# Sixteen unread products of the identity on TensorE in a fused attention and mixing kernel

## Chip, cores and metric

One core of a Trainium2 chip runs the whole kernel. The metric is the device time of one execution in microseconds, as the median of several runs.

## What is computed

Three parts follow each other: a blockwise attention over 2 batches, 8 heads, 768 positions and 64 values a head; a channel mix with a gate; and a token and channel mix. Everything is float32.

```python
# attention: a local window of 15 keys on each side, and 24 block summaries
scores = concat(where(|i - j| < 16, q k^T / 8, -1e9), q kmax^T / 8 + log(32))
a = softmax(scores)
x = a @ concat(v, vmean)
# channel mix
xk = mu_k * x + (1 - mu_k) * x_prev ;  xr = mu_r * x + (1 - mu_r) * x_prev
y = sigmoid(xr @ w_r) * (relu(xk @ w_k)**2 @ w_v)
# token mix and channel mix
u = y + (relu(y^T @ w_tok1) @ w_tok2)^T
out = u + relu(u @ w_ch1) @ w_ch2
```

## The kernel before

Attention is cut into 24 units: batch `b`, tile `t` of 128 queries, and `e`, which takes the even or the odd heads. A unit passes through four stages, each with its own place in the loop of `attention()`:

- `s_stage` (line 288): 8 score products on PE (`sp`, fp32, 64 rows, 120 columns) into a PSUM bank of tag `s` (2 of them); then for each of four head pairs DVE adds the mask and takes the minimum (`sm`, `mn`, line 307) and ACT takes the exponential (`pe`, line 310).
- `n_stage` (line 315), one unit later: DVE takes the reciprocal of the sums (`den`), POOL multiplies the four `pe` tiles (line 320).
- `t_stage` (line 323), two units later: four transposes on PE (`pt`, line 326), and a copy to `PT` by DVE in batch 0 and by ACT in batch 1.
- `v_stage` (line 334), three units later: 8 products on PE (`pv`, line 343); after the odd unit of a tile ACT copies the result to `xT` (line 348).

Between the units stands the first part of the channel mix, the generator `main()`. It handles 256 positions at a time: `mixed` makes the mixed input in two parts, high and low (`tmp` on POOL line 417, `xk` on DVE line 418, `xh` on ACT, `xl` on DVE line 420); `mm3` multiplies three times for each pair of parts (line 428), into `ko` for `w_k`, one PSUM bank of tag `ko`, and into `acc` for `w_v`. `k2_tile` squares the result in between. The weights come in as 8-byte numbers and are split by ACT, DVE and POOL (`Weights.step`, lines 133 to 158); a step is taken in every third turn of the loop from the tenth.

How attention and `main()` interleave in the program is set by a credit: each `yield` of `attention()` gives its cost times 1.2 (1.8 from the 25th on), and products of `main()` are emitted until it is used up. A scheduler then fixes the order of every engine, by priorities (`ahead`) and readiness on a timeline of its own. A product, copy or transfer can be tied with `after` behind the last score product so far (`mark`), in the order of the queues alone.

In front of the loop SP issues the loads, POOL makes the identity `ident` (line 78) and the masks, DVE takes block maxima of the keys (`ks`, line 221) and sums of the values (`vrs`, line 243), and POOL copies the maxima next to the keys (`kw`, line 227). The first score product waits for the last of these.

Behind attention come the rest of `main()`, the gate (`ro`), the token mix (`h`, `ho`) and the channel mix (`go`, `o`), which are products of 128x512 one behind the other.

Of the kernel before, what the change touches and what calls it, by code (L numbers as in the profile page):

```python
# [25 lines left out]
RATIO, NR, RATIO2 = 1.2, 25, 1.8  # L26
SIDE_EVERY = 3
AHEAD = 4
WFIRST = 2
S2COST, S3COST, S4COST = 4, 5, 4  # L30
PT_ACT = (1,)
# [18 lines left out]
def fused_kernel(ctx, tc, q, k, v, vt, mu, w_k, w_v, w_r, w_t1, w_t2, w_c1, w_c2, out):  # L50
    nc = tc.nc
# [21 lines left out]
    def bank(tag, bufs, shape, name):  # L73
        return ps.tile(shape, F32, tag=tag, bufs=bufs, name=name)

    const = pool("const", "left")
    ident = const.tile([128, 128], F32, name="ident")
# [14 lines left out]
    class Slot:  # L92


        def __init__(self, pl, tag):
            self.pl, self.tag = pl, tag
# [16 lines left out]
    class Weights:  # L113


        def __init__(self):
            self.todo, self.loaded, self.rounded, self.pin, self.ahead = [], [], [], 0, AHEAD

# [43 lines left out]
    def behind(inst, marks):  # L162

        for m in marks:
            tc.add_manual_dep(inst.ins, m.ins.name,
                              mybir.DependencyInfo(mybir.DependencyClass.NoSync, mybir.DependencyReason.DATA), reason="queue order")

    def after(inst):

        behind(inst, mark[-1:])  # L170
# [19 lines left out]
    def ahead(n):  # L190

        def wrap(fn):
            def run(*args, **kw):
                with tc.high_priority(n) if n else ExitStack():
                    return fn(*args, **kw)
            return run
        return wrap
# [3 lines left out]
    def st_of(b):  # L201
        if b not in state:
            state[b] = {"kw": {}, "qT": {}, "vw": {}, "pv": {}}
            state[b]["ks"] = at.tile([128, NP, NB], F32, tag="ks", bufs=2, name="ks")
        return state[b]
# [17 lines left out]
    @ahead(HK)  # L223
    def kw_sums(b, t):
        st = state[b]
        for o in (0, WC - NB):
            nc.gpsimd.tensor_scalar(st["kw"][t][:, :, o:o + NB], st["ks"], 1.0, 1.0, ALU.mult, ALU.mult)
# [17 lines left out]
    @ahead(HR)  # L245
    def v_gather(b):
        st = state[b]
        vp = bank("pt", 2, [128, NP, 128], "vp")
        for p in range(NP):
            nc.tensor.transpose(vp[:NB, p], st["vr"][:, p], ident)  # L250
        st["vs"] = at.tile([NB, DM], F32, tag="vs", bufs=1, name="vs")
        nc.scalar.activation(st["vs"], vp[:NB].rearrange("p g e -> p (g e)"), AF.Copy, scale=1.0 / BLOCK)

    @ahead(HL)
    def vw_load(b, t):
        ws = []
        for half in range(2):
            w = ybuf[:NC, 2 * t + half] if b == 0 else at.tile([NC, DM], F32, tag="vw", bufs=6, name="vw")
            row, srow = (NB, 0) if half == 0 else (0, NK)
            key = 128 * t + 64 * half  # L260
            after(nc.sync.dma_start(w[row:row + NK], v[b, key:key + NK]))
            ws.append((w, srow))
        st_of(b)["vw"][t] = ws

    def vw_sums(b, t):
        ahead(HV if b or t == 0 else 0)(copy_sums)(b, t)
# [12 lines left out]
    @ahead(HL)  # L279
    def q_load(b, t):  # L280
        if b == 0:
            st_of(b)["qT"][t] = xT[:, :, XB + 1 + 128 * t:XB + 129 + 128 * t]
        else:
            st_of(b)["qT"][t] = at.tile([128, NP, 128], F32, tag="qT", bufs=QB, name="qT")
        after(nc.sync.dma_start(st_of(b)["qT"][t], q[b, t]))

    @ahead(HS)
    def s_stage(u):
        b, t, e = u
        st = state[b]  # L290
        mask = masks[1 if t == 0 else 2 if t == NT - 1 else 0]
        kw, qT = st["kw"][t], st["qT"][t]
        sp = bank("s", 2, [128, NP, NC], "sp")
        mn = at.tile([128, NP], F32, tag="mn", bufs=3, name="mn")
        den = at.tile([128, NP], F32, tag="den", bufs=4, name="den")
        P = []
        r = slice(64 * e, 64 * e + 64)
        for p in range(NP):
            for half in range(2):
                c0 = half * (WC - NC)  # L300
                m = nc.tensor.matmul(sp[64 * half:64 * half + 64, p], qT[r, p, 64 * half:64 * half + 64],  # L301
                                 kw[r, p, c0:c0 + NC], start=True, stop=True)
        if PINL:
            mark.append(m)
        for p in range(NP):
            s = at.tile([128, NC], F32, tag="sm", bufs=4, name="sm")
            nc.vector.tensor_tensor_reduce(out=s, in0=sp[:, p], in1=mask, op0=ALU.add, op1=ALU.min,  # L307
                                           scale=-1.0 / math.sqrt(D), scalar=3.0e38, accum_out=mn[:, p:p + 1])
            pe = at.tile([128, NC], F32, tag="pe", bufs=12, name="pe")
            nc.scalar.activation(pe, s, AF.Exp, bias=mn[:, p:p + 1], scale=-1.0, accum_out=den[:, p:p + 1])  # L310
            P.append(pe)
        return {"u": u, "P": P, "den": den}

    @ahead(HN)
    def n_stage(z):
        den = z["den"]
        nc.vector.tensor_scalar(den, den, 1e-9, None, ALU.add)
        nc.vector.reciprocal(den, den)
        for p in range(NP):
            nc.gpsimd.tensor_scalar(z["P"][p], z["P"][p], den[:, p:p + 1], 1.0, ALU.mult, ALU.mult)  # L320

    @ahead(HT)
    def t_stage(z):
        pt = bank("pt", 2, [128, NP, 128], "pt")
        for p in range(NP):
            nc.tensor.transpose(pt[:NC, p], z["P"][p], ident)  # L326
        z["PT"] = at.tile([NC, NP, 128], F32, tag="PT", bufs=2, name="PT")
        if z["u"][0] in PT_ACT:
            nc.scalar.copy(z["PT"], pt[:NC])
        else:  # L330
            nc.vector.tensor_copy(z["PT"], pt[:NC])

    @ahead(HV)
    def v_stage(z):
        b, t, e = z["u"]
        st = state[b]
        if e == 0:
            st["pv"][t] = bank("pv", 1, [128, NP, 128], "pv")
        pv = st["pv"][t]
        for p in range(NP):  # L340
            h = 2 * p + e
            for half in range(2):
                nc.tensor.matmul(pv[64 * e:64 * e + 64, p, 64 * half:64 * half + 64],  # L343
                                 st["vw"][t][half][0][:, h * D:(h + 1) * D],
                                 z["PT"][:, p, 64 * half:64 * half + 64], start=True, stop=True)
        if e == 1:
            c0 = b * XB + 1 + 128 * t
            nc.scalar.copy(xT[:, :, c0:c0 + 128], pv)
# [5 lines left out]
    def attention():  # L354
        zs = {}
        for i in range(n_units + VLAG):
            if i < n_units:
                b, t, e = units[i]
                zs[i] = s_stage(units[i])
                yield 0.95  # L360
                if e == 1 and t + 1 < NT:
                    kw_sums(b, t + 1)
                if t == 0 and e == 1 - b:
                    if b == 0:
                        v_gather(b)
                    vw_sums(b, 0)
            if 0 <= i - 1 < n_units:
                n_stage(zs[i - 1])
            if 0 <= i - TLAG < n_units:
                t_stage(zs[i - TLAG])  # L370
                yield 0.43
            if 0 <= i - VLAG < n_units:
                v_stage(zs.pop(i - VLAG))
                yield 0.7
                done_tiles[0] = (i - VLAG + 1) // 2
            if i < n_units:
                if e == 0:
                    if t + 1 < NT and t + 1 not in state[b]["vw"]:
                        vw_load(b, t + 1)
                    if b and t + 2 < NT:  # L380
                        q_load(b, t + 2)
                elif t + 1 < NT:
                    vw_sums(b, t + 1)
                if b + 1 < B:
                    prep_next(b + 1, 2 * t + e)
# [113 lines left out]
    def drain(g):  # L499
        for _ in g:  # L500
            pass


    q_load(0, 0)
    for t in range(NT):
        k_load(0, t)
# [7 lines left out]
    for t in range(2, NT):  # L514
        for _ in range(WFIRST):
            weights.load()
# [36 lines left out]
    for n, cost in enumerate(attention()):  # L553
        weights.pin = PIN0 if n < N0 else PIN1
        if n >= W0 and n % SIDE_EVERY == 0:
            weights.step()
        credit += cost * (RATIO if n < NR else RATIO2)
        while credit > 0:
            got = next(hidden, None)
            if got is None:  # L560
                credit = 0.0
                break
            credit -= got
# [246 lines left out]
```

## Time and profile before

| | us |
|---|---|
| median of 3 runs (531.76 to 535.03) | 532.42 |
| the profiled execution | 532.74 |
| its span, first to last instruction | 530.9 |
| PE busy in the span | 504.5 |
| DVE, ACT, POOL busy | 253.5, 204.1, 203.2 |

Busy time of PE is from the start of a product to its modelled end, so groups overlap a little and a busy PE need not be at its peak. A product in fp32 leaves more than one record in the trace; these are called passes below. Times in rows count from the start of the span.

### The profile page before, as it was taken

How to read it: one execution, taken by the hardware profiler on the slowest of the kernel's cores; microseconds unless marked ns; L12 is line 12 of the kernel's file. 1: busy time of each engine (PE TensorE's matmuls, PEld its weight loads, DVE VectorE, ACT ScalarE, POOL GpSimd, SP SyncE). 2: the span in 40 equal slices, each digit the busy share in tenths (PEclk: the TensorE clock that was granted, in tenths of full speed). 3: DMA queues.
4: the chain of work that ended last, by engine and by line, in shares of the span. 5: the costliest groups of instructions: out<-in, count | busy, mean ns of one | idle time of the engine just before them, and what ended most of it. 6: DMA issues, size and time to landing. Idle time of an engine off the chain costs nothing.

```text
span 530.9 us, 7836 instructions
## 1 busy us (share of the span) xinstructions
PE 504.5 (95%) x2936; PEld 412.2 (78%) x2936; DVE 253.5 (48%) x556; ACT 204.1 (38%) x471; POOL 203.2 (38%) x298
## 2 busy tenths in 40 slices
PE   1899979999999999999999999999999999999995
PEld 1676867788888898888877788888888888888884
DVE  3976997614222466668854957443331221211112
ACT  0666656545443545455435435343310110110100
POOL 6567798934344555557741522422200000000000
PEclk9999999999999999999999999999999999999999
DMA  8999732102100850000145733000020000200002
GB/s 269 323 308 374 228 94 66 38 8 71 39 2 1 279 197 1 1 1 2 40 129 170 294 123 115 1 1 1 0 80 0 2 0 1 79 0 1 0 1 79
DMA packets 24197, 45.40 MB, mean 86 GB/s; under 512 B 2112, under 2 KB 11328, under 8 KB 24160
## 3 DMA queue, kind: packets, MB, share of 16 engines
q1 hardware_dynamic: 24160, 44.90, 26.3%
q8 instruction: 23, 0.38, 0.3%
q14 instruction: 14, 0.11, 0.1%
HBM read 41.16 MB, written 3.15 MB: 83 GB/s over the span
## 4 chain that ended last, share of the span: by engine, by line
PE 77%; DVE 9%; POOL 5%; issue 4%; ACT 2%; DMA 2%; SPq 1%; POOLq 0%; DVEq 0%; ACTq 0%
PE o L735 19%; PE go L428 19%; PE ko L428 9%; PE acc L428 8%; PE sp L301 5%; PE pv L343 4%; PE ro L428 4%; PE pt L326 3%; PE ho L428 3%; PE h L428 2%; POOL pe L320 1%; DMA xT<-in_vt_dram 1%; DVE xk L418 1%; DVE wf L147 1%; POOL tmp L417 1%
## 5 line engine op out<-in xcount | busy, mean ns | idle before, releaser
L428 PE MATMUL go<-u,w 128*128 128x512 f32 x432 | 106.7, 393 | 0.0
L156 POOL TENSOR_TENSOR w<-wf,w 128x512 fp32r<-128x512 f32 x50 | 66.1, 1325 | 88.0 <-ACT w L155 86.6
L428 PEld LDWEIGHTS go<-u,w 128*128 128x128 f32 x432 | 80.7, 188 | 17.5
L735 PE MATMUL o<-w,gh 128*128 128x512 f32 x288 | 89.0, 395 | 0.0
L650 DVE SCALAR_TENSOR_TENSOR gl<-go,gh 128x512 fp32r<-128x512 f32 x36 | 24.9, 691 | 121.1 <-ACT gh L649 121.0
L428 PE MATMUL ko<-xh,w 128*128 128x256 f32 x384 | 77.7, 288 | 0.0
L649 ACT ACTIVATE gh<-go 128x512 fp32r<-128x512 f32 x36 | 21.5, 597 | 128.8 <-PE go L428 128.7
L428 PEld LDWEIGHTS ko<-xh,w 128*128 128x128 f32 x384 | 62.1, 189 | 2.7 <-issue 0.9
L735 PEld LDWEIGHTS o<-w,gh 128*128 128x128 f32 x288 | 54.0, 188 | 12.1
L428 PE MATMUL acc<-w,kh 128*128 128x512 f32 x192 | 60.9, 401 | 0.6 <-ACT kh L442 0.6
L320 POOL TENSOR_SCALAR pe<-pe,den 128x120 f32<-128x120 f32 x96 | 46.2, 497 | 26.2 <-ACT rl L440 15.1
L735 PE MATMUL o<-w,gl 128*128 128x512 f32 x144 | 55.4, 394 | 0.0
L428 PE MATMUL ko<-xl,w 128*128 128x256 f32 x192 | 54.8, 286 | 0.1
L155 ACT CAST w<-wf 128x512 fp32r<-128x512 f32 x50 | 30.9, 618 | 52.0 <-DVE wf L153 49.6
L310 ACT ACTIVATE pe<-sm,mn 128x120 f32<-128x120 f32 x96 | 36.8, 385 | 33.9 <-DVE mn L307 27.8
L153 DVE SCALAR_TENSOR_TENSOR wf<-wst,wf 128x512 int32<-128x512 int32 x50 | 44.0, 882 | 8.9 <-ACT wst L143 6.8
L417 POOL TENSOR_SCALAR tmp<-xT,oms 128x256 f32<-128x256 f32 x52 | 32.9, 642 | 29.9 <-DVE xk L418 25.2
L443 POOL TENSOR_TENSOR kl<-rl,kh 128x512 fp32r<-128x512 f32 x24 | 33.5, 1396 | 21.6 <-ACT kh L442 13.0
L428 PEld LDWEIGHTS acc<-w,kh 128*128 128x128 f32 x192 | 34.4, 189 | 7.8 <-ACT kh L442 1.0
L418 DVE SCALAR_TENSOR_TENSOR xk<-xT,mus,tmp 128x256 f32<-128x256 f32 x52 | 34.7, 697 | 10.9 <-POOL tmp L417 10.8
L428 PE MATMUL acc<-w,kl 128*128 128x512 f32 x96 | 37.5, 402 | 0.9 <-POOL kl L443 0.9
L428 PEld LDWEIGHTS ko<-xl,w 128*128 128x128 f32 x192 | 36.2, 189 | 1.5 <-DVE xl L420 0.3
(77 smaller groups left out, 719.9 us busy)
## 6 DMA issues: line engine op xcount, KB each, us to landing
wst<-in_moe_w_ch_dram SPq DMA_DIRECT2D x24, 512.0 KB, 5.1
wst<-in_moe_w_k_dram SPq DMA_DIRECT2D x8, 512.0 KB, 9.4
wst<-in_moe_w_v_dram SPq DMA_DIRECT2D x8, 512.0 KB, 7.2
kw<-in_k_dram SPq DMA_DIRECT2D x12, 320.0 KB, 4.4
wst<-in_moe_w_tok_dram SPq DMA_DIRECT2D x6, 512.0 KB, 5.3
out_dram<-o SPq DMA_DIRECT2D x12, 256.0 KB, 2.1
ybuf<-in_v_dram SPq DMA_DIRECT2D x12, 192.0 KB, 10.6
vw<-in_v_dram SPq DMA_DIRECT2D x12, 192.0 KB, 2.8
```

The source lines that it names most:

```text
L153: nc.vector.scalar_tensor_tensor(wi, top, 3, wi, ALU.logical_shift_left, ALU.bitwise_or)
L155: self.rounded.append(nc.scalar.copy(hi, wf))
L156: nc.gpsimd.tensor_tensor(lo, wf, hi.bitcast(F32), ALU.subtract)
L301: m = nc.tensor.matmul(sp[64 * half:64 * half + 64, p], qT[r, p, 64 * half:64 * half + 64], kw[r, p, c0:c0 + NC], start=True, stop=True)
L310: nc.scalar.activation(pe, s, AF.Exp, bias=mn[:, p:p + 1], scale=-1.0, accum_out=den[:, p:p + 1])
L320: nc.gpsimd.tensor_scalar(z["P"][p], z["P"][p], den[:, p:p + 1], 1.0, ALU.mult, ALU.mult)
L417: nc.gpsimd.tensor_scalar(tmp, xT[:, d, x0 - 1:x0 - 1 + MW], om[:, d:d + 1], 1.0, ALU.mult, ALU.mult)
L418: nc.vector.scalar_tensor_tensor(xk[:, d], xT[:, d, x0:x0 + MW], mu[:, d:d + 1], tmp, ALU.mult, ALU.add)
L428: nc.tensor.matmul(o, l, r, start=(first and i == 0), stop=(last and i == 3 * n - 1))
L443: nc.gpsimd.tensor_tensor(lo, rl, hi.bitcast(F32), ALU.subtract)
L650: nc.vector.scalar_tensor_tensor(lo, o, 0.0, hi.bitcast(F32), ALU.max, ALU.subtract)
L735: nc.tensor.matmul(acc[t], l, r, start=(f == 0 and i == 0), stop=(f == nf - 1 and i == 2))
```

## The change

A function `spin(n)` is new. It takes the bank of tag `ko`, which `main()` uses later, and multiplies the identity by the identity, repeated four times, in fp32: 128 rows, 512 columns. Nothing reads the result. Eight of these are emitted ahead of all loads, and one more behind the scores of each of the first eight units. Each is tied with `after` behind the last score product so far; for the first eight there is none yet.

```diff
+SPIN0 = 8
+SPIN, SPIN_UNITS = 1, 8
...
                 zs[i] = s_stage(units[i])
+                if i < SPIN_UNITS:
+                    spin(SPIN)
                 yield 0.95
...
-
+    def spin(n):
+
+        o = bank("ko", 1, [128, 4, 128], "spin")
+        for _ in range(n):
+            after(nc.tensor.matmul(o, ident, ident.unsqueeze(1).to_broadcast([128, 4, 128]), start=True, stop=True))
+
+
+    spin(SPIN0)
     q_load(0, 0)
```

Line numbers shift by 2 in `attention()` and the functions above it, by 4 behind it and by 11 behind `spin`.

The start of PE's program before: the scores of the first two units (`sp_230`, `sp_257`), the sums of the values being transposed (`vp`), and two more units.

```order
L301 MATMUL sp_230<-kw_90,xT_84 64x120
L301 MATMUL sp_257<-kw_90,xT_84 64x120
L301 MATMUL sp_230<-kw_90,xT_84 64x120 x7
L301 MATMUL sp_257<-kw_90,xT_84 64x120 x7
L250 MATMUL vp_286<-ident_61,vrs_224 24x128 x2
L301 MATMUL sp_303<-kw_92,xT_84 64x120 x8
```

The same place now, up to the third of the single products.

```order
L511 MATMUL spin_88<-ident_61 128x512 x8
L303 MATMUL sp_239<-kw_99,xT_84 64x120
L303 MATMUL sp_268<-kw_99,xT_84 64x120
L303 MATMUL sp_239<-kw_99,xT_84 64x120 x7
L303 MATMUL sp_268<-kw_99,xT_84 64x120 x4
L511 MATMUL spin_266<-ident_61 128x512
L303 MATMUL sp_268<-kw_99,xT_84 64x120 x3
L252 MATMUL vp_299<-ident_61,vrs_233 24x128 x2
L303 MATMUL sp_316<-kw_101,xT_84 64x120 x8
L511 MATMUL spin_295<-ident_61 128x512
L303 MATMUL sp_358<-kw_101,xT_84 64x120 x8
L511 MATMUL spin_343<-ident_61 128x512
```

(A second pair of `vp`, which stands ahead of `sp_358`, is left out.) The eight stand ahead of everything, and single ones between the scores of the first units. All sixteen stand ahead of the first `ko` of `main()`.

Further on the order of PE is another one too. In batch 1, around the scores of its third tile, it was this before (`sp_1579` and `sp_1670` are scores, `acc` and `ko` products of `main()`):

```order
L428 MATMUL acc_1424<-w_773,kh_1417 128x512 x2
L428 MATMUL acc_1424<-w_773,kl_1418 128x512
L301 MATMUL sp_1579<-kw_785,qT_1215 64x120 x8
L301 MATMUL sp_1670<-kw_980,qT_1387 64x120
L326 MATMUL pt_1709<-ident_61,pe_1489 120x128
L428 MATMUL ko_1606<-xh_1152,w_1036 128x256
```

Now the scores of the third tile (`sp_1604`) stand here:

```order
L328 MATMUL pt_1467<-ident_61,pe_1259 120x128
L303 MATMUL sp_1604<-kw_810,qT_1240 64x120 x6
L328 MATMUL pt_1467<-ident_61,pe_1263 120x128
L303 MATMUL sp_1604<-kw_810,qT_1240 64x120 x2
L345 MATMUL pv_1477<-PT_1379,vw_1120 64x64
L345 MATMUL pv_1477<-PT_1379,vw_1122 64x64
```

Where products of `main()` stood on both sides of these scores, there are now transposes and value products of other units: batch 1 stands closer together, and more of `ko` and `acc` stands behind it.

## Rows read from the trace of the kernel before

**Rows 1.** The page's part 2: the span in 40 slices, busy tenths and granted clock.
```profile
PE   1899979999999999999999999999999999999995
PEclk9999999999999999999999999999999999999999
```

**Rows 2.** Windows by stage; columns as the heading row names them.
```profile
core 0: us, PE busy (x) PEld busy (x) DVE busy (x) ACT busy (x) POOL busy (x), PEclk, DMA share, GB/s
21.80:38.00 16.20, 15.75 (x111) 12.31 (x111) 12.47 (x42) 10.26 (x35) 12.85 (x25) 1.00 1.08 317
38.00:58.30 20.30, 20.01 (x128) 14.44 (x128) 15.13 (x60) 13.68 (x45) 16.29 (x25) 1.00 0.90 300
58.30:62.50 4.20, 4.20 (x60) 3.73 (x60) 4.20 (x13) 3.16 (x11) 3.58 (x6) 1.00 0.91 306
62.50:87.70 25.20, 22.14 (x200) 18.53 (x198) 22.44 (x57) 13.50 (x34) 20.25 (x31) 1.00 0.48 128
87.70:184.70 97.00, 96.32 (x770) 78.28 (x769) 38.23 (x140) 48.31 (x142) 52.19 (x81) 1.00 0.18 58
```

**Rows 3.** Timeline of PE: start, length in us, instruction, passes, [idle before].
```profile
53.99 3.31 PE L343 MATMUL pv<-PT,ybuf 120*64 120x64 f32 x32
57.23 1.11 PE L326 MATMUL pt<-ident,pe 128*120 128x128 f32 x4
...
59.39 1.15 PE L343 MATMUL pv<-PT,ybuf 120*64 120x64 f32 x16
60.47 0.65 PE L326 MATMUL pt<-ident,pe 128*120 128x128 f32 x4
...
62.54 0.36 PE L428 MATMUL ko<-xh,w 128*128 128x256 f32 x1
...
69.99 0.85 PE L326 MATMUL pt<-ident,pe 128*120 128x128 f32 x3 [1.56 <-DVE den L317]
70.77 1.15 PE L343 MATMUL pv<-PT,ybuf 120*64 120x64 f32 x16
...
90.23 0.33 PE L326 MATMUL pt<-ident,pe 128*120 128x128 f32 x1
```

**Rows 4.** The chain that ended last: start, us on it, what.
```profile
21.83 0.47 PE pt L326
22.30 1.80 PE sp L301 x16
...
32.00 1.90 PE pv L343 x16
...
51.06 0.63 DVE PT L331
...
97.19 0.56 PE sp L301 x8
...
108.82 1.07 PE pv L343 x16
```

**Rows 5.** The chain from 21.8 to 51.1 us, shares by line.
```profile
by line: PE sp L301 42.0%; PE pv L343 29.3%; PE pt L326 20.8%; DVE PT L331 4.2%; DVE wf L153 2.1%; issue 1.8%; DVE sm L307 1.0%; ACT pe L310 0.7%; DVE mn L307 0.0%
```

**Rows 6.** Groups on PE from 21.8 to 58.3 us: passes, busy us, mean ns, idle before.
```profile
L301 PE MATMUL sp<-kw,xT 64*64 64x120 f32 x112 | 15.6, 416 | 0.0
L343 PE MATMUL pv<-PT,ybuf 120*64 120x64 f32 x96 | 12.5, 320 | 0.7 <-DVE PT L331 0.7
L326 PE MATMUL pt<-ident,pe 128*120 128x128 f32 x31 | 10.7, 444 | 0.3 <-POOL pe L320 0.3
```

**Rows 7.** Timeline of the first 15 us: identity, first scores, first sum of values.
```profile
1.11 0.29 POOL masks.py:199 TENSOR_SCALAR_AFFINE_SELECT ident<-ident 128x128 f32<-128x128 f32 x1
...
11.73 2.95 PE L301 MATMUL sp<-kw,xT 64*64 64x120 f32 x32 [11.73 <-POOL kw L227]
...
13.38 1.75 DVE L243 TENSOR_REDUCE vrs<-xT 128x48 f32<-128x1536 f32 x1 [2.14 <-DMA xT<-in_vt_dram]
```

**Rows 8.** Waits of DVE from 21.8 to 62.5 us: us in total, times, longest.
```profile
DVE PT L331 <- PE pt L326: 4.6, 2, 2.4
DVE sm L307 <- ACT pe L310: 3.6, 3, 2.8
```

## The prediction

> **What bounds the kernel now.** I read the page's parts 1 and 2 first, then windows by stage, then the PE timeline where its durations change, and then the chain of waits. PE is busy for nine tenths or more of nearly every slice behind the first, and its clock row shows the same top digit in all 40 [rows 1]. [...] The reader is to distrust that row here, because the durations on PE do not fit it. Sixteen passes of `pv` take 1.90 us in the chain at 32.00 us and 1.07 us at 108.82 us; sixteen passes of `sp` take 1.80 us at 22.30 us, and eight take 0.56 us at 97.19 us [rows 4]. The change falls between two neighbours of one kind: four `pt` take 1.11 us at 57.23 us and 0.65 us at 60.47 us, and `pv` x16 at 59.39 us is already short [rows 3]. A single `pt` takes 0.47 us early [rows 4] and 0.33 us late [rows 3], a good part of it a fixed latency, so the step of one more is (1.11 - 0.47)/3 = 0.213 us against (0.65 - 0.33)/3 = 0.107 us: a factor of two, which is the distance between the two clock levels. So I read it thus: PE runs at the low level from its first product to about 58.3 us and at the high one from there on. Transfers do not explain it: the DMA share is 0.90 in the slow stage before 58.3 us and 0.91 in the fast one behind it [rows 2].
>
> What PE did before the rise: it was busy for 20.01 of 20.30 us [rows 2], with products on 64 columns and transposes, and the last thing of note is a run of 32 `pv` [rows 3]. So mere occupancy did not raise the clock in this kernel.
>
> [...]
>
> Then the chain. From 21.8 to 51.1 us it lies on PE: `sp`, `pv` and `pt` hold 42.0 + 29.3 + 20.8 = 92% of these 29.3 us, or 27.0 us [rows 5]. At 51.06 us it goes over to DVE [rows 4], which has the first mixed tile to make; the first dense `ko` product starts at 62.54 us [rows 3]. From 87.7 to 184.7 us PE is busy 96.32 of 97.00 us [rows 2]; a shift that arrives there lasts to the end.
>
> **The front: eight products.** They wait for the identity alone, whose last step begins at 1.11 us and takes 0.29 us [rows 7], so they start near 1.5 us. No row shows a full 128x512 fp32 product. By the step of `pt` (128 columns in one pass, 0.213 or 0.107 us) 512 columns take 0.85 or 0.43 us a pass; the trace shows two passes for each fp32 `sp` product (32 passes for 16 instructions [rows 7]), so I take 1.71 us slow and 0.86 us fast for one. At one pass it would be half of that; two fits the other fp32 products of the kernel. Eight then take 6.9 us (all fast) to 13.7 us (all slow): they end at 8.4 to 15.2 us, and at 11.8 us if half of their work is fast. The first `sp` starts at 11.73 us today [rows 7], so half-fast is free. All slow would hold `sp` for 3.5 us, but DVE is in a 1.75 us reduction until 15.1 us [rows 7] and starts on the scores only then, so that at most some 2 us would reach the chain. I take 0, with 2 us as the other end.
>
> **The eight further products.** In the new order of PE eleven of the sixteen stand ahead of the first `pt`: the front and three more. There the chain runs over DMA, DVE, ACT and POOL, and PE has room (it is not on the chain until 21.83 us [rows 4]); I cost these three at nothing, and at 2.6 us if that cover is gone. The other five lie in the stretch where PE is the chain: 5 x 0.86 = 4.3 us fast, 8.6 us slow. Each writes the bank of `ko` and is read by nobody; the first real `ko` stands behind all sixteen, so no `ko` waits for a reader of theirs.
>
> **What the clock gives back.** Between 21.8 and 58.3 us the trace has 112 passes of `sp`, 96 of `pv` and 31 of `pt` [rows 6]. With steps from the chain [rows 4]: `sp` 0.1125 - 0.070 = 0.0425 us x 112 = 4.8 us; `pv` 0.119 - 0.067 = 0.052 us x 96 = 5.0 us; `pt` 0.213 - 0.107 = 0.106 us x 31 = 3.3 us. Sum 13.1 us of PE work in a stretch where PE is busy 35.8 us [rows 2]. On the chain are 27.0 of these: 13.1 x 27.0/35.8 = 9.9 us. Less the five products, 9.9 - 4.3 = 5.6 us. If all of it counted (PE alone is the limit up to 58.3 us), it would be 13.1 - 4.3 = 8.8 us.
>
> **Whether the others can follow.** In 21.8 to 62.5 us DVE waited 4.6 us for `pt` and 3.6 us for `pe` [rows 8], together 8.2 us; POOL was busy 12.85 + 16.29 of 36.5 us up to 58.3 us [rows 2], so it has 7.4 us. Both have more than 5.6 us and less than 8.8 us: the room bears the first figure and not the second. The stretch behind it, 62.5 to 87.7 us, holds DVE at 22.44 and POOL at 20.25 of 25.2 us [rows 2]; nothing is won there, but a start 5.6 us earlier is kept if the work ahead of it is the same.
>
> **The order.** It is not the same. The scheduler places batch 1 earlier on PE: between the twelfth and the twenty-second unit's `pv` there stand 108 `ko` and 36 `acc` products, where before there were 204 and 104. Ahead of the first `xl` DVE has 6 weight splits instead of 8, and 6 key reductions instead of 9. All of it has to be done before the dense stage anyway, so I count 0, with a loss of up to 8 us (the rival below) and a gain of up to 3 us (idle time of PE in 62.5 to 87.7 us [rows 2] that better filling could close) as the ends.
>
> **Sum.** The profiled execution took 532.74 us, of which 530.9 us are the span; the median of the three runs shown is 532.42 us, 0.3 us less, so the sum may be read against either. 532.74 - 5.6 = 527.1 us.
>
> **Rivals.** *All of the low clock comes back.* If DVE and POOL fill their waits fully and the filling behind improves by those 3 us, the gain is 8.8 + 3 = 12 us: 521 us. For it: no engine has more busy time up to 58.3 us than PE. Against it: DVE and POOL have only 8.2 and 7.4 us to give, at different moments.
>
> *The gain is hidden.* DVE carries the chain from 51.06 us; if it is the limit earlier too, its waits turn from waits for PE into waits for ACT's `pe` and POOL, and 1 us remains: 532 us. For it: the 3.6 us of waits for `pe` are not PE's own [rows 8].
>
> *The clock does not rise, or falls back between units.* Then each of the eight costs 1.71 us: 8.6 us in the PE stretch plus some 1 us at the start, 542 us. Place: PE, 21.8 to 51.1 us. It decides if four `pt` still take 1.11 us in that stretch. For it: the products between the spins are the ones that did not raise the clock before. Against it: once up, it stayed up over a PE wait of 1.56 us; the `pv` behind that wait are short again [rows 3].
>
> [...] The pause between the front and the first `sp` is up to 3.3 us by the ends above; no run here shows a pause of that length in the fast stage.
>
> *The bunched batch 1 costs more than the clock gives.* In 62.5 to 87.7 us, where attention is dense, PE idles 3.06 of 25.2 us, 12%; behind it 0.68 of 97 us [rows 2]. If 12% holds for the next 70 us of the new order, that is 8.3 us more; with half the gain, 532.74 - 2.8 + 8.3 = 538 us. It decides if PE's idle time from 90 to 160 us is over 6 us.
>
> **How the numbers follow.** 1% is 5.3 us, about what a measurement of this kernel can tell from no change. Chances: the forecast (gain of 3 to 9 us) 0.45, all comes back 0.18, hidden 0.17, clock low 0.10, bunching 0.10. Faster by over 1%: some 0.30 of the forecast's 0.45, and the 0.18: 0.48. Slower by over 1%: the last two but for a little, 0.18. Within 1%: 0.34. The range reaches from 518 us (all comes back and some more) to 539 us (bunching in full); the forecast's own range is 523.5 to 530 us.
>
> **What would show it.** In the changed profile: the first eight products from about 1.5 us, the later of them half as long as the first; four `pt` in 0.65 us from the first unit on; sixteen `sp` passes in some 1.1 us (twice the 0.56 us of eight) at 22 us; the first `ko` near 57 us and not 62.54 us; from 190 us on the same rows as before, some 5 to 6 us earlier. The prediction is wrong if `pt` is still long after 12 us, if the first `ko` comes no earlier, or if it comes earlier and PE then stands idle between 80 and 160 us.

## The result and the profile after

The changed kernel takes 521.15 us (median of 4 runs, 520.51 to 521.76); the kernel before took 532.76 us beside it (4 runs). The ratio is 0.9772, 95% interval 0.9754 to 0.979: 11.6 us less, about twice the 5.3 us (1%) that the prediction puts as what a measurement can tell from no change. The forecast was 527.1 us; the direction was right, and the size is that of the first rival (521 us). Where executions of one kernel below spread by more than 1.5%, its ratio counts those near its fastest alone, and the median counts all.

The profiled execution took 520.51 us, its span is 518.7 us, 12.2 less than before. The page's part 2 of the changed kernel, which answers to [rows 1]:

```profile
PE   8997889999999999999999999999999999999995
PEclk9899999999999999999999999999999999999998
```

PE now works from the first slice on. Its clock row shows one step down in the second slice and one in the last, where the row before had none at all; and yet this is the kernel with the faster PE. The timeline of PE says why (start, length in us, instruction, passes, [idle before]); it answers to [rows 3, 7]:

```profile
1.46 9.96 PE L511 MATMUL spin<-ident 128*128 128x512 f32 x16 [1.46 <-POOL ident masks.py:199]
11.84 1.33 PE L303 MATMUL sp<-kw,xT 64*64 64x120 f32 x26 [0.42 <-POOL kw L229]
...
15.31 0.39 PE L252 MATMUL vp<-ident,vrs 128*24 128x128 f32 x2 [0.53 <-DVE vrs L245]
16.27 1.04 PE L303 MATMUL sp<-kw,xT 64*64 64x120 f32 x16 [0.57 <-issue]
17.23 1.92 PE L511 MATMUL spin<-ident 128*128 128x512 f32 x2
18.95 0.63 PE L252 MATMUL vp<-ident,vrs 128*24 128x128 f32 x2
19.51 1.67 PE L303 MATMUL sp<-kw,xT 64*64 64x120 f32 x16
21.11 1.13 PE L511 MATMUL spin<-ident 128*128 128x512 f32 x2
22.07 0.38 PE L328 MATMUL pt<-ident,pe 128*120 128x128 f32 x2
22.39 1.04 PE L303 MATMUL sp<-kw,xT 64*64 64x120 f32 x16
23.35 0.65 PE L328 MATMUL pt<-ident,pe 128*120 128x128 f32 x4
...
27.04 1.90 PE L345 MATMUL pv<-PT,ybuf 120*64 120x64 f32 x32
...
53.52 0.39 PE L432 MATMUL ko<-xh,w 128*128 128x256 f32 x1 [0.82 <-ACT xh L423]
...
191.82 1.11 PE L432 MATMUL ro<-w,xh 128*128 128x512 f32 x4
```

Sixteen `sp` passes take 1.04 us where they held the chain for 1.80 [rows 4], four `pt` 0.65 where they took 1.11, 32 `pv` 1.90 where they took 3.31 [rows 3]. Only from 17.4 to 20.9 us are they long again (`sp` 1.67 us, a single product 1.92). The front itself, cut where the trace records its first change of clock (7.19 us), the products alone:

```profile
core 0: us, PE busy (x) PEld busy (x), PEclk, DMA share, GB/s
1.40:7.19 5.79, 5.73 (x7) 2.52 (x8) 1.00 0.86 247
7.19:11.50 4.31, 4.23 (x10) 1.52 (x8) 1.00 1.14 327
```

Seven passes fill the first 5.73 us, 0.82 us each; ten fill 4.23 us, 0.42 us each. The clock column says 1.00 on both sides of a factor of two: it shows the fall that comes later in this execution (0.51 from 17.40 to 20.90 us, below), and not the low level at which the execution begins. That is how the clock row of before could show nothing of a PE that ran at half speed from 11.73 to 58.6 us (the step of one `pt` more was 0.213 us, and 0.107 us behind it). Whoever reads that row reads durations beside it.

By stage (columns as in [rows 2]):

```profile
17.40:20.90 3.50, 3.50 (x18) 1.86 (x20) 2.60 (x21) 2.93 (x14) 0.89 (x4) 0.51 1.10 321
...
21.80:53.50 31.70, 27.22 (x306) 19.68 (x303) 26.56 (x118) 24.29 (x84) 27.84 (x50) 1.00 1.07 335
...
53.50:80.00 26.50, 23.29 (x206) 19.07 (x207) 25.58 (x56) 17.04 (x46) 24.99 (x37) 1.00 0.64 178
80.00:191.80 111.80, 111.80 (x887) 95.58 (x886) 50.87 (x152) 58.08 (x152) 64.16 (x86) 1.00 0.23 80
```

The 12.2 us are made in two places. The first `ko` starts at 53.52 us and not at 62.54 [rows 3], 9.0 us earlier. From there to the first `ro` it is 191.82 - 53.52 = 138.3 us, and was 141.4 (that `ro` started at 203.97): 3.1 us less, in a stretch that was already at the high level before. Behind it both kernels need the same 327 us.

The first part can be taken apart. From 21.8 us to the first `ko` there were 40.70 us with PE busy 15.75 + 20.01 + 4.20 = 39.96 [rows 2]; there are 31.70 with PE busy 27.22. The groups on PE in the two stretches (passes, busy us, mean ns, idle before), first from 21.8 to 62.5 us of before, where [rows 6] end at 58.3, then from 21.8 to 53.5 us now:

```profile
L301 PE MATMUL sp<-kw,xT 64*64 64x120 f32 x128 | 16.4, 398 | 0.0
L343 PE MATMUL pv<-PT,ybuf 120*64 120x64 f32 x128 | 14.8, 296 | 0.7 <-DVE PT L331 0.7
L326 PE MATMUL pt<-ident,pe 128*120 128x128 f32 x38 | 11.9, 415 | 0.3 <-POOL pe L320 0.3
```

```profile
L345 PE MATMUL pv<-PT,ybuf 120*64 120x64 f32 x128 | 8.7, 225 | 3.7 <-DVE PT L333 2.8 <-ACT wst L145 0.9
L303 PE MATMUL sp<-kw,xT 64*64 64x120 f32 x128 | 8.1, 270 | 0.0
L328 PE MATMUL pt<-ident,pe 128*120 128x128 f32 x38 | 6.8, 286 | 0.0
L511 PE MATMUL spin<-ident 128*128 128x512 f32 x12 | 6.7, 636 | 0.0
```

So both stretches hold the same work, but for the products. The chain of waits in the new one, by line:

```profile
by line: POOL pe L322 26.9%; PE spin L511 19.4%; issue 13.4%; PE sp L303 11.7%; POOL w L158 7.9%; PE pv L345 5.8%; POOL tmp L421 5.5%; PE pt L328 3.6%; DVE sm L309 3.4%; DVE PT L333 1.9%; ACT pe L312 1.6%; DVE den L320 0.3%; DVE den L319 0.
```

PE held 92% of the chain [rows 5]. Now POOL holds the largest share, and PE's largest is that of the products themselves: 19.4% of 31.7 us, 6.1 us. Without them PE's busy time is 27.2 - 6.1 = 21.1 us, 18.9 less than before. PE idles 4.48 us where it idled 0.74: 3.7 more. The balance is 18.9 - 6.1 - 3.7 = 9.1 us, against 9.0 seen (an account of one pair of stretches, which has to close; the 6.1 us are the chain's share and not a busy time).

DVE's waits in the same stretch answer to [rows 8]:

```profile
DVE sm L309 <- ACT pe L312: 4.6, 2, 3.7
DVE PT L333 <- PE pt L328: 0.3, 1, 0.3
```

Its waits for `pt` went from 4.6 to 0.3 us and those for `pe` grew by 1.0: together 3.3 us less, though the stretch is 9.0 us shorter. The rest is busy time that is gone from the stretch: DVE's fell from 31.8 [rows 2] to 26.6 us, POOL's from 32.7 to 27.8. In it are two weight splits and three key reductions fewer on DVE and three weight splits fewer on POOL.

### The profile page after: what moved, and what is told of

Same layout as the page of the kernel before. It is cut to its first block, busy times and chain, and to the rows that moved or that the text cites. A ratio compares the mean times of both kernels' runs of the same rounds, so it can differ in the third digit from the quotient of the medians.

```text
span 518.7 us, 7924 instructions
## 1 busy us (share of the span) xinstructions
PE 500.0 (96%) x2968; PEld 405.6 (78%) x2968; DVE 250.7 (48%) x556; ACT 204.2 (39%) x471; POOL 205.2 (40%) x298
## 4 chain that ended last, share of the span: by engine, by line
PE 80%; POOL 7%; issue 4%; DVE 3%; DMA 2%; ACT 2%; SPq 1%; POOLq 0%; DVEq 0%; ACTq 0%
PE o L746 19%; PE go L432 19%; PE ko L432 11%; PE acc L432 10%; PE ro L432 5%; PE pv L345 3%; PE sp L303 3%; PE ho L432 3%; POOL pe L322 3%; PE h L432 2%; PE pt L328 2%; POOL w L158 2%; PE spin L511 2%; POOL tmp L421 1%; DMA xT<-in_vt_dram 1%
## 5 line engine op out<-in xcount | busy, mean ns | idle before, releaser
L432 PE MATMUL acc<-w,kh 128*128 128x512 f32 x192 | 59.8, 401 | 0.7 <-ACT kh L446 0.6
L447 POOL TENSOR_TENSOR kl<-rl,kh 128x512 fp32r<-128x512 f32 x24 | 34.6, 1443 | 34.8 <-ACT kh L446 32.6
L421 POOL TENSOR_SCALAR tmp<-xT,oms 128x256 f32<-128x256 f32 x52 | 34.0, 664 | 33.1 <-DVE xk L422 23.9
L445 DVE TENSOR_TENSOR rl<-rl 128x512 f32<-128x512 f32 x24 | 19.6, 818 | 46.2 <-ACT rl L444 46.2
```

Of the source, the lines that this page charges most:

```text
L421: nc.gpsimd.tensor_scalar(tmp, xT[:, d, x0 - 1:x0 - 1 + MW], om[:, d:d + 1], 1.0, ALU.mult, ALU.mult)
L432: nc.tensor.matmul(o, l, r, start=(first and i == 0), stop=(last and i == 3 * n - 1))
L447: nc.gpsimd.tensor_tensor(lo, rl, hi.bitcast(F32), ALU.subtract)
```

## Experiments

The theory: PE starts at the low level and stays there through attention's thin products; the sixteen products bring the high level early and help to hold it, and that is the gain. Rivals: the gain is the scheduler's new order; or part of the sixteen (the front, or the single ones) does it all. Every edit below is made to the changed kernel. No part of the required computation is left out, but each edit also lets the scheduler choose another order, so runs are read by their clock and their landmarks too. How like two orders are is counted on PE's passes ahead of the first `ko`, products left out: of the changed kernel's 362, 313 stand in one sequence with those of before (364).

**The front alone (e1) and the single products alone (e2).**

```diff
-SPIN, SPIN_UNITS = 1, 8
+SPIN, SPIN_UNITS = 1, 0
```

> Only the eight products in front, none behind the units (SPIN_UNITS 0). Theory A, the low clock was the whole loss and PE sets the pace up to the first ko: the clock rises near 7 us and, if it stays up, the first ko comes 4.3 us earlier than in the changed kernel (about 49 us), the time is 517 us; if it falls back for good at the thin stretch behind the first scores, the first ko comes near 62 us and the time is 531 us. Theory B, DVE and POOL set the pace once PE is fast: the clock stays up and the first ko stays at 53 to 54 us, the time at 520 to 522 us. Theory C, most of the gain is the new order and not the clock: the order of this kernel is nearer to that of before, and the time is 526 us or more although pt is fast.

```diff
-SPIN0 = 8
+SPIN0 = 0
```

> Only the eight single products, none in front (SPIN0 0). Theory A: PE starts slow; if single products among the scores raise the clock at all they do so late, each costs 1.71 us until then, and the time lies between 525 and 538 us; the later the rise, the slower. Theory B: the same, with less lost. Theory C (order): 519 to 523 us although pt takes 0.213 us a step, since the order is nearer to that of the changed kernel.

Measured: e1 530.1 us, ratio 0.9945 (0.9924 to 0.9966); e2 530.77 us, ratio 0.9948 (0.9933 to 0.9963). Windows of e1, cut where its clock changes:

```profile
15.50:39.40 23.90, 21.53 (x164) 16.88 (x164) 19.40 (x94) 17.62 (x68) 16.13 (x33) 0.50 1.08 304
39.40:53.00 13.60, 11.02 (x130) 8.16 (x128) 13.45 (x41) 10.45 (x35) 12.46 (x18) 1.00 1.04 363
53.00:59.90 6.90, 5.43 (x37) 4.38 (x37) 6.90 (x18) 3.85 (x12) 6.02 (x9) 0.51 1.10 350
```

The front raised the clock at 5.3 us, but it fell at 15.5 us and stayed low for 23.9 us with PE busy 21.53 of them. In e2 the three earliest products take 1.92 to 2.07 us, and the first rise comes at 30.8 us. Alone the parts gain 3.3 us (533.35 - 530.1) and 2.6 us; together 11.6. Neither is enough by itself: the front brings the high level 24 us sooner than the single products do (7.19 us in the changed kernel, 30.8 us in e2), and with them it lasts, but for 3.4 us, to 191.8 us, where in e1 it was lost for 23.9 us at once. The first `ko` misleads here: in e1 it comes at 53.69 us, as in the changed kernel, but with 324 passes ahead of it and not 362, and the first `ro` comes at 201.44 us. So this landmark compares two kernels only where the same work stands ahead of it.

**The same places, hardly any work: one row (e7), 64 columns (e9), one column (e10).**

```diff
-nc.tensor.matmul(o, ident, ident.unsqueeze(1).to_broadcast([128, 4, 128]), ...
+nc.tensor.matmul(o, ident[:1], ident[:1].unsqueeze(1).to_broadcast([1, 4, 128]), ...
```

> The same sixteen products with one row of the identity as both operands and not 128: as many columns, as long on PE, with one row of the array at work. If rows count for the clock, it does not rise in front and falls or stays low later: the front ends near 15 us and the time is 533 us or more (theory A and B); an order theory says 522 to 528 us in spite of it. If only the columns passed count, the clock behaves as in the changed kernel and the time is 520 to 526 us, by the order.

```diff
-nc.tensor.matmul(o, ident, ident.unsqueeze(1).to_broadcast([128, 4, 128]), ...
+nc.tensor.matmul(o[:, 0, :64], ident, ident[:, :64], ...
```

> The sixteen products at the same places with 64 columns and not 512, an eighth of the work; the scheduler's order on PE is nearer to that of the changed kernel than to that of before. Clock theory (A): the front is over in some 2 us, the clock stays low through the scores, the first ko comes at 58 to 63 us and the time is 531 to 537 us. Order theory (C): 522 to 527 us with slow transposes.

```diff
-nc.tensor.matmul(o, ident, ident.unsqueeze(1).to_broadcast([128, 4, 128]), ...
+nc.tensor.matmul(o[:, 0, :1], ident, ident[:, :1], ...
```

> The same sixteen with a single column: no work to speak of, and a third order of the scheduler, unlike both. Clock theory (A): slow as before, 530 to 536 us, and what it differs from before is what the order alone does at a low clock; a spread of over 3 us between this one, the one with 64 columns and before says that order is worth as much. Order theory (C): anything.

Measured: e7 546.55 us, ratio 1.026 (1.0245 to 1.0275); e9 534.93 us, 1.0031 (1.0009 to 1.0054); e10 535.53 us, 1.0033 (1.0007 to 1.0059). PE's timeline, first of e7, then of e9:

```profile
1.46 14.02 PE L511 MATMUL spin<-ident 1*128 1x512 f32 x16 [1.46 <-POOL ident masks.py:199]
15.41 0.87 PE L303 MATMUL sp<-kw,xT 64*64 64x120 f32 x8
...
74.69 0.58 PE L432 MATMUL ko<-xh,w 128*128 128x256 f32 x1
```

```profile
1.46 3.67 PE L511 MATMUL spin<-ident 128*128 128x64 f32 x16 [1.46 <-POOL ident masks.py:199]
...
52.08 1.11 PE L328 MATMUL pt<-ident,pe 128*120 128x128 f32 x4
...
61.40 0.36 PE L432 MATMUL ko<-xh,w 128*128 128x256 f32 x1
```

In e7 the products run through one row of the array, and all sixteen passes of the front are slow: 14.02/16 = 0.88 us each. The first rise is recorded at 47.5 us, and the kernel lies 25.4 us behind the changed one: it pays the products at the low level and gets nothing for them. In e9 the front is short, four `pt` still take 1.11 us at 52 us, and the first `ko` comes at 61.40 us; e10 rises at 59.3 us. Both have products in all the places of the change, and none of the gain. They don't show what the changed kernel's order does at the low level, since theirs is another one: 288 of e9's 323 passes ahead of the first `ko` stand in one sequence with the changed kernel's and 293 with those of before. For e10 the late first `ko` (68.38 us) shows that an order by itself can cost some us.

**Transposes of the same columns (e3).** Each product becomes eight transposes of 128 columns.

```diff
-            after(nc.tensor.matmul(o, ident, ident.unsqueeze(1)...
+            for i in range(4):
+                for _ in range(2):
+                    after(nc.tensor.transpose(o[:, i], ident, ident))
```

> Each unread product is replaced by eight unread transposes of the identity with the same number of columns passed (the order of the rest is near that of the changed kernel). If transposes raise the clock as products do: front of 1.7 us a group at first, then 0.86, time 519 to 524 us. If they do not: PE stays slow, the front ends near 15 us, each later group costs 1.71 us, and theory A and B say 535 to 545 us; theory C (order) says 522 to 528 us in spite of the slow clock.

Measured: 525.19 us, ratio 0.9832 (0.9812 to 0.9852). The front's transposes in e3, cut at its first change of clock:

```profile
1.46:6.86 5.40, 5.40 (x26) 5.40 (x27) 1.00 0.81 218
6.86:11.30 4.44, 4.42 (x40) 4.18 (x39) 1.00 1.13 321
```

26 take 5.40 us (0.208 each), the next 40 take 4.42 (0.111 each). Transposes raised the clock as the products did (6.86 and 7.19 us). The executions spread from 523.55 us (mean clock 0.995) to 530.11 (0.985): the slower the execution, the more low clock is recorded in it. The profiled one is the slowest, with a fall from 23.9 to 30.8 us.

Ahead of the first `ko` this order is nearly the changed kernel's (358 of 362 passes in one sequence), so e3 is the nearest that the runs come to one order at two clock levels. From the scores of the fifth unit to the seven `pt` behind those of the eighth both kernels give PE the same work (64 passes of `sp`, 32 of `pv`, six of `pt` and five of the groups that replace or are single products), and PE has next to no gap. The changed kernel first, then e3:

```profile
22.39:33.72 11.33, 11.33 (x113) 7.12 (x113) 8.33 (x36) 7.91 (x24) 10.82 (x21) 1.00 1.08 311
```

```profile
23.76:39.40 15.64, 15.58 (x144) 12.71 (x144) 6.59 (x31) 7.63 (x23) 12.14 (x25) 0.78 1.08 299
...
59.40 0.38 PE L432 MATMUL ko<-xh,w 128*128 128x256 f32 x1 [0.56 <-ACT xh L423]
```

With 6.8 us of it at the low level the stretch takes 4.3 us more, which is most of the 5.9 us by which the first `ko` is later than 53.52 us.

**Six single products, two behind each of the first three units (e4), and products of half the width, sixteen of them in front (e8).**

```diff
-                if i < SPIN_UNITS:
-                    spin(SPIN)
+                if i in (0, 1, 2):
+                    spin(2)
```

> Eight in front, and two behind each of the first three units, none later (14 products and not 16, nearer to the start). In the changed kernel the clock fell at 17.4 us and rose again at 20.8 us, behind a stretch in which PE did little. Theory A: with more in that stretch the clock does not fall (or rises sooner), 1.5 us of slow passes go, and two products are saved: 517 to 520 us. If the clock falls for good once the products end: 526 us or more. Theory B: 520 to 522 us.

```diff
-SPIN0 = 8
+SPIN0 = 16
...
-nc.tensor.matmul(o, ident, ident.unsqueeze(1).to_broadcast([128, 4, 128]), ...
+nc.tensor.matmul(o[:, :2], ident, ident.unsqueeze(1).to_broadcast([128, 2, 128]), ...
```

> Products of half the columns (256): sixteen in front, so the same work there, and one half product behind each of eight units, 0.43 us each and not 0.86. If the half products still keep the clock up: theory A 519 us (2.1 to 3.4 us less), theory B 520 to 522 us. If they are too thin, the clock falls between the units and the time is 525 to 533 us, with a spread between executions as in the kernel with two behind each of three units.

Measured: e4 535.05 us as median, but ten executions of the one program lie between 525.82 and 539.01 us (ratio 0.9913, 0.9868 to 0.9957, by the fastest). e8 533.21 us (528.82 to 535.79), ratio 1.0 (0.9975 to 1.0026). Windows of e4's profiled execution (527.0 us), at its two falls:

```profile
37.80:44.60 6.80, 6.61 (x53) 5.80 (x51) 3.60 (x20) 4.54 (x17) 3.87 (x7) 0.50 1.04 320
65.10:71.90 6.80, 4.73 (x22) 4.73 (x23) 6.80 (x8) 2.76 (x4) 3.57 (x5) 0.50 0.41 94
```

Its front raised the clock at 7.1 us. It fell some 13 us behind the last of the six, right after a wait of PE of 1.56 us, and stayed low for 6.8 us although PE was busy for 6.61 of them; the second fall came within a wait of 5.84 us. In e8 it rose at 6.3 us and was low again from 16.5 to 37.0 us. Since e4 is one program with one order, its spread is the cleanest measure of the clock: the execution of 525.82 us has a mean clock of 0.985, that of 539.01 us 0.958. The recorded low level is half of the high one (`PEclk` 0.50 against 1.00 in e1's and e4's windows), so they have about 2 x 0.015 x 526 = 16 and 2 x 0.042 x 539 = 45 us of it recorded; 13.2 us more for 29 us of low clock is about 0.45 us for each; a line through all ten gives 0.38. The mean leaves out the low level ahead of the first rise, so such a figure serves only kernels that rise early: in e10, where the profiled execution rises at 59.3 us, 535.1 us goes with a mean of 0.973 and 538.14 us with 0.994.

**How many: two behind each unit (e6), twelve units (e5), seven (e11), nine (e12).**

```diff
-SPIN, SPIN_UNITS = 1, 8
+SPIN, SPIN_UNITS = 2, 8
```

> Two products behind each of the first eight units and not one (8 in front). Eight more products are 6.9 us of PE at the high clock. Theory A: if PE sets the pace, five of the eight units stand in its chain, 4.3 to 6.9 us more, 525 to 528 us. Theory B: POOL and DVE hide most of it, the first ko stays at 53 to 56 us, 521 to 524 us, and the fall of the clock at 17 us is gone.

```diff
-SPIN, SPIN_UNITS = 1, 8
+SPIN, SPIN_UNITS = 1, 12
```

> Eight in front, one behind each of the first twelve units and not eight. Theory A (every us of low clock costs about half a us, and the four later products cost 0.86 us each where PE is the chain): the clock stays up as in the changed kernel, 524 to 525 us, 3.4 us over it. Theory B (up to the first ko POOL and DVE set the pace once PE is fast, so more products cost little): 521 to 522 us. If the later ones keep the clock from a fall that the changed kernel still has now and then, 519 to 521 us.

```diff
-SPIN, SPIN_UNITS = 1, 8
+SPIN, SPIN_UNITS = 1, 7
```

> One product behind each of the first seven units and not eight. Theory A (each product lies on the path up to the first ko with its full 0.86 us): 520.3 us, 0.86 us less than the changed kernel, if the clock holds; with a fall of 6.8 us somewhere 523 to 524 us. Theory B: 521 us, no difference.

```diff
-SPIN, SPIN_UNITS = 1, 8
+SPIN, SPIN_UNITS = 1, 9
```

> One behind each of the first nine units; of all orders tried this one is nearest to that of the changed kernel. Theory A: 522.0 us, 0.86 us more, with the first ko at 54.4 us if the ninth stands ahead of it. Order theory: within 1 us of the changed kernel if only the order matters, 521 us.

Measured: e6 531.53 us, ratio 0.9972 (0.9954 to 0.9989; two of its ten executions took 622.33 and 2800.45 us, which no trace here explains); e5 525.56 us, 0.9874 (0.9816 to 0.9932); e11 527.11 us, 0.9871 (0.985 to 0.9892); e12 526.89 us, 0.9881 (0.986 to 0.9901). e6, e11 and e12 miss every time that was expected of them. The first `ko` of e6, of e5 and of e12:

```profile
60.37 0.36 PE L432 MATMUL ko<-xh,w 128*128 128x256 f32 x1
```

```profile
53.54 0.39 PE L432 MATMUL ko<-xh,w 128*128 128x256 f32 x1 [0.82 <-DMA kw<-in_k_dram]
```

```profile
54.28 0.39 PE L432 MATMUL ko<-xh,w 128*128 128x256 f32 x1 [0.82 <-ACT xh L423]
```

Eight more products put the first `ko` of e6 6.85 us later than the changed kernel's, up to 0.86 us for each, if its other order counts nothing (310 of 360 passes in one sequence). It has a fall from 23.6 to 27.0 us in that stretch, as the changed kernel has one from 17.4 to 20.8.

Ahead of the first `ko` e5 and e12 have the changed kernel's order pass for pass and eight single products like it; the further ones stand behind. Neither has a fall there. e5's first `ko` does not move: its first scores start 0.6 us later, and by 23.86 us, where the changed kernel is at 23.84, it stands at the same product. So of the changed kernel's fall at 17.4 us little or nothing is left in its time. e12's is 0.8 us later, as its first scores were (12.63 us against 11.84). So with this order and the high level the early first `ko` comes again, within 0.8 us.

Behind it the kernels part. In e5 the first `ro` comes 3.0 us later, and the profiled execution, without a fall up to 194.8 us, has a span of 521.5 us, 2.8 more than the changed kernel's: 0.75 us for each of the four further products, if the order counts nothing. But e12, with one further product, needs 143.65 us from the first `ko` to the first `ro` against 138.3, so the order counts here, and the price isn't shown. Seven and nine units are slower than eight too, by 6.0 and 5.7 us in the medians, of which 1.0 us is the kernel before, slower by that beside these runs (533.77 us). Falls are in both profiled executions: three of 3.4 us in e11 (from 12.9, 57.3 and 135.8 us), one in e12 (from 135.0 us), about 1.5 us each by e4's measure. What remains is put down to the order by subtraction alone. No run was faster than the changed kernel.

## Why the prediction was right in direction and short in size

*The low clock up to 58 us, read from durations against the clock row.* Right. The trace of before records its first change of clock, a rise, at 58.62 us; after, the same passes are half as long from 22 us on. The two levels that the clock column records are 1.00 and 0.50 (e1, 15.5 to 39.4 us), the factor of two that the step of `pt` gave. DMA was rightly left out: its share in the fast 21.8 to 53.5 us is 1.07, no lower than in the slow stages of before (1.08 and 0.90 [rows 2]).

*The front, counted 0.* Right: first `sp` at 11.84 us, was 11.73. The front ended at 11.42 us (1.46 + 9.96), near the 11.8 worked out for half of the work fast, with passes of 0.82 and 0.42 us where 0.85 and 0.43 were put.

*Three further products hidden at 0, five at 4.3 us.* Too low. The first `pt` starts 1.0 us later (22.07, was 21.08), with a fall of the clock there; and the five with the end of a sixth hold 6.1 us of the chain. From its start to that of the next instruction each of the five takes 0.86 to 1.06 us, where 0.86 was put.

*What the clock gives back: 13.1 us of work, of which 27.0/35.8 counts.* This is the step that failed, as a size: the 13.1 us. The term for `sp` sets sixteen slow passes (1.80 us) against eight fast ones (0.56 us), in which the start of the group weighs more; sixteen fast ones take 0.96 us from start to start (16.27 to 17.23 us), so the step is 0.052 us and not 0.0425. And a step inside a long run is not what a pass of a short group loses. By the groups a pass went from 15.6/112 = 0.139 us to 8.1/128 = 0.063 us for `sp`, 0.130 to 0.068 for `pv`, 0.345 to 0.179 for `pt` [rows 6]: the start of each short group, counted as fixed, shrank too (a single `pt` took 0.47 us early and 0.33 us late [rows 3, 4]). PE gave back 18.9 us, not 13.1. Some of that may be the order, which has the same 38 `pt` in 13 groups where there were 18. An estimate says how much the level alone makes of it: with before's slow durations on the chain (1.80 us for sixteen `sp`, 1.90 for sixteen `pv`, 0.47 for a first `pt` [rows 4], 0.213 for each further one) the new order's 128, 128 and 38 passes would take some 41 us; they took 21.1. The plain reading, half of the 35.8 us of slow busy time, 17.9, would have been closer. The discount was about right: 3.2 us were taken off by the share of the chain, and 3.7 us came as new idle time of PE. So 18.9 - 6.1 - 3.7 stands where 13.1 - 3.2 - 4.3 stood.

*Whether the others can follow.* The limit set by 8.2 us of DVE and 7.4 us of POOL did not hold, because it took their work ahead of the first `ko` as given. In the new order DVE is busy 5.2 us and POOL 4.9 us less there. That this is paid later, where it costs less, is argued: from 53.5 to 80 us DVE is busy 25.58 of 26.5 us and PE idles 3.2, about what it idled at that place before (3.06 [rows 2]); from 80 to 191.8 us PE is busy all 111.80 us.

*The order, counted 0 with a gain of 3 us as one end.* Between the first `ko` and the first `ro` 3.1 us were gained, at the high level in both kernels, so the order is what is left to explain them. PE's idle time between the first `ko` and the first `ro` went from 4.06 to 3.19 us, and its busy time from 137.4 to 135.1 for the same 1090 passes; `pt` stands in some 40 groups there where it stood in some 50. That the grouping saves the 2.3 us is argued from these counts. It is luck too: in all the other runs here this stretch takes between 140.96 us (e10) and 147.75 us (e1). Ahead of the first `ko` e3 shows one order at two levels for part of the way; no run holds the new order at the low level throughout, so what the order alone is worth there stays open.

*The rivals.* "All of the low clock comes back" came in its figures, 8.8 and 3 us (9.0 and 3.1 measured), with some luck: its 8.8 is 13.1 - 4.3, where 18.9 - 6.1 - 3.7 was measured, and DVE and POOL did not fill their waits but had less to do. "Hidden" fell: DVE's waits for `pt` went and those for `pe` grew, in the direction that it said but by 1.0 us only, and 9 us remained. "The clock falls back between units" came for 3.5 us only (17.4 to 20.9 us, `PEclk` 0.51). Its counterargument, a clock that stayed up over a wait of 1.56 us, was weaker than it looked (and its 542 us lay outside the range given, 518 to 539): in e4 the clock fell behind a wait of the same 1.56 us. "The bunched batch 1" had the wrong sign: its test was over 6 us of PE idle time from 90 to 160 us, and there is none from 80 on (12% of 70 us is 8.4 and not 8.3 us, which moves nothing).

*What raised the level, and what ended it.* That dense products would raise it was the author's estimate; no row of before shows a 128x512 product in the slow stage. The runs bear it out (7.19 us in the changed kernel). Transposes stood among the work that left the level low before: PE was busy 35.8 us from 21.8 to 58.3 us [rows 2, 6] without a rise. In e3 transposes of the identity raised it at 6.86 us, so to be a transpose was not by itself what kept it low. The pause between the front and the first `sp`, put at up to 3.3 us, was 0.42 us. The clock fell at 17.4 us behind pauses of 0.42, 0.53 and 0.57 us, and in e12 at 135.0 us behind none, so a long pause was not what did it there. The falls of e1 and e4 did come behind or within waits of 1.56 to 5.84 us.

## What to carry to other kernels

Compare the duration of one and the same small product early and late in the trace before you believe the clock row: here a factor of two (0.213 and 0.107 us a step of `pt`) was the clock, and half of the 35.8 us of PE's busy time at the low level, 17.9 us, was a fair first estimate of the 18.9 us that PE gave back. Raising the level and holding it were two things here; the front alone and the single products alone gave 3.3 and 2.6 us, both 11.6, of which some 3 us are the order. Unread work was paid where PE was the limit (0.86 to 1.06 us a product), so its number is found by runs, and where a scheduler sets the order, every edit near it brings a new order worth some us either way.

## What the runs showed of the hardware that was not expected

In the changed kernel the clock column reads 1.00 from the start of the execution past the first recorded change (7.19 us), with passes of 0.82 us ahead of it and of 0.42 us behind it under the same 1.00. The mean clock of before's profiled execution, whose PE was at half speed up to 58.6 us, is 0.999.

PE busy all the time was not enough to raise or to hold the level. In e7 one-row products kept PE busy for 14.02 us, and PE was busy for all the 32.09 us from there to 47.5 us, without a rise; products through all 128 rows raised it at 7.19 us. Once low it stayed so with PE busy 21.53 of 23.9 us (e1) and 6.61 of 6.80 us (e4). What stood ahead of a fall differed: waits of PE of 1.83 and 1.72 us in e1 (15.5 us), one of 1.56 us in e4 (37.8 us), and in e12 none, where it fell at 135.0 us behind `ko` in turn with short groups of `pv`:

```profile
128.20:135.00 6.80, 6.80 (x52) 5.41 (x52) 0.00 (x0) 0.28 (x1) 0.00 (x0) 1.00 0.00 0
```

Executions of one program differ in their falls: e4 from 525.82 to 539.01 us at mean clocks of 0.985 and 0.958, e5 from 523.26 (no fall up to 194.8 us, 0.998) to 530.11 us (0.982). The changed kernel's own stay within 1.3 us of each other, one of them with a mean clock of 0.999 at 520.8 us, the profiled one with 0.994 at 520.51.
